# Values of the other half copied by ScalarE, chunk 22 through DRAM, and a new order: sliding-window attention with sinks and a gated layer, on one core

## The chip, the cores and the metric

The kernel runs on one core of a Trainium2 chip. The metric is the device time of one execution in microseconds (us), as the median over runs of the same program. In the text and in the rows PE is TensorE (PEld its weight loads, which overlap its matmuls), DVE is VectorE, ACT is ScalarE, POOL is GpSimd and SP is SyncE, which issues all of this kernel's transfers.

## The reference

Two parts, one behind the other. The first is attention over 4 batches x 8 heads x 768 positions x 64 elements, in which a position sees the last `window` = 128 positions and the first `n_sink` = 4:

```python
scores = np.matmul(q, k.transpose(0, 1, 3, 2)) / np.sqrt(D)
keep = (pos[None, :] < n_sink) | ((rel >= 0) & (rel < window))
scores = np.where(keep, scores, -1e9)
a = np.exp(scores - scores.max(-1, keepdims=True))
x = np.matmul(a / (a.sum(-1, keepdims=True) + 1e-9), v)
```

The second takes the 3072 rows of 512 elements through a layer of 1024:

```python
h = x @ w_in
e = np.exp(h - h.max(-1, keepdims=True))
solu = h * e / (e.sum(-1, keepdims=True) + 1e-9)
ln = (solu - mu) / np.sqrt(var + 1e-6) * g_ln
out = ln @ w_out
```

`w_in`, `w_out` and `g_ln` come as 8-byte floating-point numbers and are converted in the kernel.

## The kernel before

The 3072 rows are worked in 24 chunks of 128, six for each batch; the chunks (0, 0) and (1, 0) come first, then the others batch by batch. Every chunk passes the same stages, each a small function:

- `load_k`, `load_q`, `load_v` bring the inputs. Chunks 0 to 6 have q and k turned on PE (`turn_q`, `turn_k`, `take_q`, `take_k`); from chunk 7 on VectorE turns them in blocks of 32 (L539, L552).
- `score` (L579) multiplies q with the keys of the chunk before, the sinks and the chunk itself, `pick` and `mask` (L596, L609) choose and mask on VectorE, `exps` (L618) is on ScalarE, and `normalise` (L639) on POOL.
- From chunk 5 on the weights p are turned by way of DRAM: `store_p`, `load_p`, `flip_p` (L667, VectorE). POOL then cuts them into the parts that belong to the new and the old values (`part_new` L692, `part_old` L705).
- `value` (L760) multiplies the parts with the values. For a chunk that is not the first of its batch (17 chunks from chunk 5 on) it works by quarters and needs the values of the other half of the partitions too: the tile `vm`, of which there is one buffer, holds the upper half of the old values in its lower partitions and the lower half of the new ones in its upper partitions. `load_mid` (L504) fills it with two transfers from SBUF to SBUF.
- `x_hi` (ScalarE) and `x_lo` (VectorE) split the result in a high and a low part, `hidden` (L799) multiplies them with the first weights: 8 steps of three matmuls. `highest` (L804), `solu_exp` (L809), `solu` (L814), `centre` (L827, L830) and `square` are the gating and the norm.
- The product u must be turned. For most chunks it goes through DRAM: `store_u`, `load_u` (four transfers), `flip_u` (L856, two on VectorE). For the first and the last chunks, those that `direct(n)` names, PE turns it: `turn_u`, four steps of two transposes (L865).
- `u_hi` (L872), `u_lo` (L876), `project` (L890, 8 steps of three matmuls; 16 narrow ones for chunk 23), `scale`, `store`.

At the start the weights are converted in 16 blocks: ScalarE lowers them (L386), VectorE moves the bits (L390, L394, L400), and high and low parts are made, those of the second weights by `w_hi` on ScalarE and `w_lo` (L429) on VectorE.

The scores, the turned q and k, the turned p, the `value` results and the turned u share two PSUM buffers (`banks`). The hidden product `h` has one buffer: `hidden` of a chunk can begin when `solu` of the chunk before has read it.

The order of the work is written out by hand: `steps` lists every function call of every chunk, and the table `ORDER` says in which order they are recorded. Each engine, SP too, works through its instructions in that order, and one that waits holds up those behind it.

Of the kernel before, what the change touches and what calls it, by code (L numbers as in the profile page):

```python
# [184 lines left out]
def _banded(ctx, tc, q, k, v, n_sink, window, w_in, w_out, g_ln, out, val, wts, wpool, consts):  # L185
# [314 lines left out]
    def load_mid(n, i):  # L500
        if ("vm", n) not in st:
            st["vm", n] = sb.tile([P, H, D], F32, tag="vm", name=f"vm_{n}", bufs=1)
        src = st["vn", n] if i else old_values(n)
        nc.sync.dma_start(st["vm", n][ROWS[i]], src[ROWS[1 - i]])  # L504
# [336 lines left out]
    def direct(n):  # L841
        return n < 2 or n >= NCH - 2
# [272 lines left out]
```

## Time and profile before

| | |
|---|---|
| median of 3 runs | 410.08 us (409.6 to 411.29) |
| the profiled execution | 409.73 us |
| its span | 408.0 us, 12392 instructions |
[...]
| busy: PE, PEld | 388.5 us (95%), 308.9 us (76%) |
| busy: VectorE, ScalarE, POOL | 302.5 (74%), 254.2 (62%), 168.7 us (41%) |
| moved by DMA | 80.82 MB |

The span is the time from the first to the last instruction; 1.7 us of the execution lie around it. Busy shares are means over stages with different limits, so the sections below read them stretch by stretch. The granted clock is half of full speed in one stretch only, between 18.6 and 25.4 us, and at the very end.

### The profile page before, as it was taken

The numbers are of one execution on the slowest core, as the hardware profiler recorded it, in microseconds if no ns is written. First come the engines' busy times: TensorE is split into PE (matmuls) and PEld (weight loads), VectorE is DVE, ScalarE is ACT, GpSimd is POOL, SyncE is SP. The second block draws the span as 40 slices with busy tenths as digits, with TensorE's granted clock in tenths as the row PEclk, the third lists the DMA queues.
The fourth block names the chain that finished last, engine by engine and source line by source line (L and its number), as shares of the span: only waits on it lengthen the run. The fifth ranks groups of instructions, "written<-read, shape, count | busy, mean of one in ns | idle before, by whom it ended". The sixth has DMA issues, their size and how long they took to land.

```text
span 408.0 us, 12392 instructions
## 1 busy us (share of the span) xinstructions
PE 388.5 (95%) x4772; PEld 308.9 (76%) x4772; DVE 302.5 (74%) x883; ACT 254.2 (62%) x698; POOL 168.7 (41%) x312
## 2 busy tenths in 40 slices
PE   3799999989989999999999999999999999999995
PEld 3564767777777887878778878888888888888885
DVE  3889999999989898987989788775645836444320
ACT  3989998874968586538557847475445445342532
POOL 6622262645463954561246763542824421010100
PEclk9979999999999999999999999999999999999999
DMA  7999539969969969889957897998686341452011
GB/s 236 308 275 319 142 81 199 178 209 242 239 178 285 225 213 286 240 182 199 307 177 246 233 236 234 259 260 241 180 243 207 106 141 77 144 167 90 28 51 58
DMA packets 83316, 80.82 MB, mean 198 GB/s; under 512 B 45868, under 2 KB 66740, under 8 KB 83252
## 3 DMA queue, kind: packets, MB, share of 16 engines
q1 hardware_dynamic: 83252, 79.98, 72.4%
q8 instruction: 39, 0.64, 0.7%
q14 instruction: 25, 0.20, 0.2%
HBM read 48.76 MB, written 26.87 MB: 185 GB/s over the span
## 4 chain that ended last, share of the span: by engine, by line
PE 76%; DVE 10%; ACT 5%; POOL 2%; issue 2%; DMA 2%; SPq 1%; DVEq 0%; ACTq 0%; POOLq 0%
PE o L890 30%; PE h L799 28%; PE banks L579 7%; PE banks L760 6%; DVE w2l L429 2%; DVE sc L609 2%; ACT sc L618 1%; PE av L770 1%; DMA wraw<-in_moe_w_in_dram 1%; POOL pt L705 1%; DVE keys L552 1%; POOL pc L692 1%; DVE wbits L400 1%; PE banks L676 1%; ACT wps L386 1%
## 5 line engine op out<-in xcount | busy, mean ns | idle before, releaser
L618 ACT ACTIVATE sc<-sc,nmx 128x132 f32<-128x132 f32 x192 | 75.6, 398 | 17.8 <-DVE nmx L609 17.5
L890 PE MATMUL o<-w2h,uh 128*128 128x512 f32 (+1 forms) x200 | 79.3, 397 | 0.0
L799 PE MATMUL h<-w1h,xh 128*128 128x512 f32 x192 | 77.8, 405 | 0.0
L890 PE MATMUL o<-w2l,uh 128*128 128x512 f32 (+1 forms) x200 | 77.1, 386 | 0.1
L890 PE MATMUL o<-w2h,ul 128*128 128x512 f32 (+1 forms) x200 | 77.1, 386 | 0.0
L799 PE MATMUL h<-w1h,xl 128*128 128x512 f32 x192 | 75.6, 394 | 0.0
L799 PE MATMUL h<-w1l,xh 128*128 128x512 f32 x192 | 75.3, 392 | 0.0
L639 POOL TENSOR_TENSOR pn<-sc,rs 128x512 f32<-128x512 f32 x38 | 42.1, 1122 | 24.0 <-DVE rs L624 9.5
L809 ACT ACTIVATE e<-h,nm 128x1024 f32<-128x1024 f32 x24 | 26.8, 1117 | 35.1 <-DVE nm L804 34.9
L609 DVE CUSTOM_DVE_ANT_0 sc<-banks,bias 128x132 f32<-128x132 f32 x192 | 46.3, 286 | 2.9 <-POOL sn L646 0.6
L692 POOL TENSOR_SCALAR_AFFINE_SELECT pc<-pt 64x512 f32<-64x512 f32 x34 | 26.7, 785 | 49.3 <-DVE pt L667 48.2
L890 PEld LDWEIGHTS o<-w2h,uh 128*128 128x128 f32 x200 | 37.6, 188 | 9.8 <-issue 1.5
L890 PEld LDWEIGHTS o<-w2h,ul 128*128 128x128 f32 x200 | 37.5, 187 | 8.5 <-issue 0.3
L799 PEld LDWEIGHTS h<-w1h,xh 128*128 128x128 f32 x192 | 36.1, 188 | 10.2 <-issue 2.4
L804 DVE TENSOR_REDUCE nm<-h 128x1 f32<-128x1024 f32 x24 | 29.2, 1216 | 19.5 <-PE h L799 19.3
L890 PEld LDWEIGHTS o<-w2l,uh 128*128 128x128 f32 x200 | 37.5, 188 | 7.3
L876 DVE TENSOR_TENSOR ul<-ur,uh 128x512 fp32r<-128x512 f32 x40 | 28.3, 717 | 19.6 <-ACT uh L872 19.6
L579 PE MATMUL banks<-keys,q 32*64 32x200 f32 (+3 forms) x1280 | 39.0, 336 | 3.8 <-ACT keys L560 1.5
L799 PEld LDWEIGHTS h<-w1h,xl 128*128 128x128 f32 x192 | 36.1, 188 | 8.1
L799 PEld LDWEIGHTS h<-w1l,xh 128*128 128x128 f32 x192 | 36.2, 188 | 7.0
L579 PEld LDWEIGHTS banks<-keys,q 32*64 32x64 f32 (+1 forms) x1280 | 28.4, 135 | 13.3 <-issue 4.4
L872 ACT CAST uh<-ur 128x512 fp32r<-128x512 f32 x40 | 24.1, 614 | 21.7 <-DVE ur L856 16.5
(154 smaller groups left out, 745.8 us busy)
## 6 DMA issues: line engine op xcount, KB each, us to landing
ud<-u SPq DMA_DIRECT2D x20, 512.0 KB, 4.2
ub<-ud SPq DMA_DIRECT2D x80, 128.0 KB, 3.7
pd<-pn SPq DMA_DIRECT2D x19, 512.0 KB, 4.2
pb<-pd SPq DMA_DIRECT2D x76, 128.0 KB, 4.2
vn<-in_v_dram SPq DMA_DIRECT2D x24, 256.0 KB, 4.6
out_dram<-ob SPq DMA_DIRECT2D x23, 256.0 KB, 2.6
kn<-in_k_dram SPq DMA_DIRECT2D x12, 384.0 KB, 6.7
qn<-in_q_dram SPq DMA_DIRECT2D x12, 384.0 KB, 7.1
```

Of the source, the lines that this page charges most:

```text
L579: nc.tensor.matmul(st["s", n, g][ROWS[y], x, 256 * j + at:256 * j + at + wide], st["q", n][rows, m, ROWS[y]], kk[rows, m].rearrange("p b x ...
L609: nc.vector.tensor_tensor_reduce(out=st["sc", n][:, h], in0=st["s", n, g][:, x, 256 * j + BLK:256 * j + BLK + SEG], in1=bias0 if c == 0 el ...
L618: nc.scalar.activation(sc[:, h], sc[:, h], AF.Exp, bias=nmx[:, h:h + 1], scale=-1.0, accum_out=ssum[:, h:h + 1])
L639: nc.gpsimd.tensor_tensor(to[:, i], st["sc", n][:, :, PARTS[i]].rearrange("p h (b x) -> p h b x", x=32), st["rs", n].unsqueeze(2).unsqueez ...
L692: nc.gpsimd.affine_select(st["pc", n][ROWS[hb]].rearrange("p h (c t) -> p h c t", c=2), old_part(n)[ROWS[hb]], pattern=[[0, H], [32, 2], [ ...
L760: nc.tensor.matmul(acc[ROWS[x], y, r, :], vals[ROWS[y], h, :], p[ROWS[y], h, :], start=False, stop=(r, i) == (NPAIR - 1, 2))
L799: nc.tensor.matmul(st["h", n][:, cols], a[:, kt, :], w[:, kt, cols], start=(kt == 0 and m == 0), stop=(kt == KT1 - 1 and m == 2))
L804: nc.vector.tensor_reduce(nm, st["h", n], axis=AX.X, op=ALU.max, negate=True)
L809: nc.scalar.activation(e, st["h", n], AF.Exp, bias=st["nm", n], scale=1.0, accum_out=se)
L872: nc.scalar.copy(uh, turned_u(n, g4))
L876: nc.vector.tensor_tensor(ul, turned_u(n, g4), st["uh", n, g4].bitcast(F32), op=ALU.subtract)
L890: nc.tensor.matmul(st["o", n, i], a[:, kt % 4, :], part(w, kt)[:, i * wide:(i + 1) * wide], start=(kt == 0 and m == 0), stop=(kt == KT2 - ...
```

## The change

Three things. `load_mid` copies by ScalarE what two transfers moved. `direct` no longer names chunk 22, so that only chunk 23 of the last ones is turned on PE, and chunk 22 has `store_u`, four `load_u` and two `flip_u` in place of four `turn_u`. And the table `ORDER` is another one throughout (2021 steps instead of 2018). Of the table two lines stand here for all.

```diff
 ORDER = (
-    143, 12, 3, 0, 5, 6, 13, 144, 146, 8, 10, 11, 15, 16, 17, 147, 148, 149, 282, 150, 151, 18, 19, 21, 153, 4, 20,
...
         src = st["vn", n] if i else old_values(n)
-        nc.sync.dma_start(st["vm", n][ROWS[i]], src[ROWS[1 - i]])
+        nc.scalar.copy(st["vm", n][ROWS[i]], src[ROWS[1 - i]])
...
     def direct(n):
-        return n < 2 or n >= NCH - 2
+        return n < 2 or n >= NCH - 1
```

What the new table moves is seen in the order of the instructions on an engine. In the rows the number behind a tile's name is the chunk (for `wps`, `wraw` and `wbits` the weight block), the last number a running one.

ScalarE at the start, before:

```order
L226 CAST ident_r_93<-ident_88 128x128
L273 COPY val_58<-spread_0_144 128x2
L386 ACTIVATE wps_0_183<-wraw_0_181 128x512
L556 COPY q_0_190<-banks_0_86 128x512
L560 COPY keys_122<-banks_0_86 128x4x2x64
L416 CAST w1h_62<-wbits_0_211 128x4x128
L404 ACTIVATE minus_218<-ident_88 128x128
```

and after the change:

```order
L226 CAST ident_r_93<-ident_88 128x128
L404 ACTIVATE minus_137<-ident_88 128x128
L386 ACTIVATE wps_0_152<-wraw_0_135 128x512
L273 COPY val_58<-spread_0_148 128x2
L416 CAST w1h_62<-wbits_0_174 128x4x128
L556 COPY q_0_181<-banks_0_86 128x512
L560 COPY keys_122<-banks_0_86 128x4x2x64
```

The cast of the first weight block (L416), which needs VectorE's three steps on that block, stands ahead of the copies of q and keys of chunk 0 instead of behind them. On SP the fetch of that block is now the first transfer.

VectorE ahead of `hidden` of chunk 5, whose `h` buffer is free when `solu` of chunk 4 (L814) has run, before:

```order
L667 STREAM_TRANSPOSE pt_6_1742<-pb_6_1385 128x1024
L609 ISA sc_10_1648,nmx_10_1649<-banks_1_87,bias2_111 128x132
L609 ISA nmx_10_1649 128x1
L856 STREAM_TRANSPOSE ur_2_0_1761<-ub_2_1677 128x512
L804 TENSOR_REDUCE nm_4_1765<-h_4_1618 128x1
L731 TENSOR_TENSOR skt_6_1769<-skp_6_1753,mine_119 128x512
L609 ISA sc_10_1648,nmx_10_1649<-banks_1_87,bias2_111 128x132
L609 ISA nmx_10_1649 128x1
L784 TENSOR_TENSOR xl_5_1774<-banks_0_86,xh_5_1767 128x2x4x64
L814 SCALAR_TENSOR_TENSOR u_4_1811,nmu_4_1812<-h_4_1618,e_4_1808 128x1024
L856 STREAM_TRANSPOSE ur_2_1_1828<-ub_2_1677 128x512
```

and after the change:

```order
L609 ISA sc_10_1656,nmx_10_1657<-banks_1_87,bias2_111 128x132
L609 ISA nmx_10_1657 128x1
L552 STREAM_TRANSPOSE keys_122<-kn_2_1340 128x4x2x16 x4
L804 TENSOR_REDUCE nm_4_1718<-h_4_1583 128x1
L552 STREAM_TRANSPOSE keys_122<-kn_2_1340 128x4x2x16 x4
L784 TENSOR_TENSOR xl_5_1782<-banks_0_86,xh_5_1779 128x2x4x64
L731 TENSOR_TENSOR skt_6_1786<-skp_6_1777,mine_119 128x512
L814 SCALAR_TENSOR_TENSOR u_4_1828,nmu_4_1829<-h_4_1583,e_4_1825 128x1024
```

Two key transposes (of the third batch, chunks 13 and 14) now stand in this stretch, the `flip_u` of chunk 2 stands behind it, and the masks of chunk 10 all stand ahead of the sinks of chunk 6 (L731).

ScalarE between the `value` results of chunks 8 and 9 (their `x_hi`, L776), before:

```order
L776 CAST xh_8_2432<-banks_1_87 128x2x4x64
L618 ACTIVATE sc_13_2117,ssum_13_2119<-sc_13_2117,nmx_13_2118 128x132 x4
L872 CAST uh_3_1_2462<-ur_3_1_2362 128x512
L618 ACTIVATE sc_14_2309,ssum_14_2311<-sc_14_2309,nmx_14_2310 128x132 x6
L776 CAST xh_9_2543<-banks_1_87 128x2x4x64
```

and after the change:

```order
L504 COPY vm_8_2382<-vn_8_2272 64x512
L504 COPY vm_8_2382<-vn_7_1879 64x512
L618 ACTIVATE sc_13_2150,ssum_13_2152<-sc_13_2150,nmx_13_2151 128x132 x4
L776 CAST xh_8_2448<-banks_1_87 128x2x4x64
L872 CAST uh_3_0_2454<-ur_3_0_2380 128x512
L504 COPY vm_9_2465<-vn_9_2032 64x512
L504 COPY vm_9_2465<-vn_8_2272 64x512
```

The copies of chunk 9 stand behind `x_hi` and `u_hi` and can begin when `value` of chunk 8 has read the one `vm` buffer.

## Rows read from the trace of the kernel before

**Rows 1.** The page, part 1: busy us (share of the span) and instructions

```profile
PE 388.5 (95%) x4772; PEld 308.9 (76%) x4772; DVE 302.5 (74%) x883; ACT 254.2 (62%) x698; POOL 168.7 (41%) x312
```

**Rows 2.** Busy time by stretch; columns in the first line

```profile
core 0: us, PE busy (x) PEld busy (x) DVE busy (x) ACT busy (x) POOL busy (x), PEclk, DMA share, GB/s
...
10.40:84.60 74.20, 67.50 (x810) 48.73 (x802) 70.07 (x225) 67.38 (x200) 31.27 (x53) 0.95 0.87 215
84.60:115.00 30.40, 29.37 (x474) 23.15 (x474) 28.80 (x114) 21.82 (x76) 14.90 (x27) 1.00 0.94 221
115.00:170.00 55.00, 54.90 (x938) 43.95 (x938) 51.28 (x177) 37.19 (x122) 31.91 (x53) 1.00 0.83 244
170.00:330.00 160.00, 159.36 (x2184) 129.25 (x2185) 118.58 (x312) 93.31 (x248) 74.44 (x125) 1.00 0.82 221
```

**Rows 3.** The chain that ended last: start us, us, what

```profile
81.88 0.68 DVE ul L876
82.64 0.59 ACT uh L872
...
84.64 1.61 PE banks L579 x64
...
359.97 0.87 PE banks L865 x8
...
374.74 9.08 PE o L890 x39
```

**Rows 4.** Waits from 84 to 408 us: who for whom, us, times, longest

```profile
PEld banks L760 <- POOL pt L705: 1.4, 4, 0.5
...
PE banks L579 <- POOL d L819: 1.2, 1, 1.2
```

**Rows 5.** Timeline of the start: start us, us, engine, line, operation, tiles [idle before]

```profile
2.55 1.05 SPq L374 DMA_DIRECT2D wraw<-in_moe_w_in_dram  x2
...
7.44 0.63 ACT L386 ACTIVATE wps<-wraw 128x512 f32<-128x512 f32 x1 [1.39 <-DMA wraw<-in_moe_w_in_dram]
...
8.10 0.70 DVE L390 TENSOR_SCALAR wps<-wps 128x512 int32<-128x512 int32 x1 [2.37 <-ACT wps L386]
8.48 0.58 ACT L560 COPY keys<-banks 128x512 f32<-128x512 f32 x1
...
10.46 0.29 DVE L609 CUSTOM_DVE_ANT_0 sc<-banks,bias 128x132 f32<-128x132 f32 x1 [0.21 <-POOL bias L279]
```

**Rows 6.** VectorE, groups by form (count, busy us, mean ns), and one timeline row

```profile
L856 DVE STREAM_TRANSPOSE ur<-ub 128x512 f32<-128x512 f32 x40 | 27.0, 694 | 5.7 <-issue 3.5 <-DMA ub<-ud 2.1
...
L552 DVE STREAM_TRANSPOSE keys<-kn 128x128 f32<-128x128 f32 x72 | 19.3, 392 | 0.0
...
113.51 0.69 DVE L731 TENSOR_TENSOR skt<-skp,mine 128x512 fp32r<-128x512 f32 x1 [0.77 <-PE skp L726]
```

**Rows 7.** ScalarE's cast out of SBUF; the `vm` transfers; SP's waits for them

```profile
L872 ACT CAST uh<-ur 128x512 fp32r<-128x512 f32 x40 | 24.1, 614 | 21.7 <-DVE ur L856 16.5 <-PE o L890 4.3 <-DVE rs L623 0.9
...
vm<-vn SPq DMA_DIRECT2D x33, 128.0 KB, 3.2
...
SPq L504 <- PE banks L760: 20.5, 5, 4.8
```

**Rows 8.** `w_lo` on VectorE (ns min/median/max), one of them, POOL at that time

```profile
L429 DVE SCALAR_TENSOR_TENSOR w2l<-wbits,g_sb,w2h x8: 666/887/1535, 52.0 to 79.4; 128x512 fp32r<-128x512 f32 x8
...
79.36 1.47 DVE L429 SCALAR_TENSOR_TENSOR w2l<-wbits,g_sb,w2h 128x512 fp32r<-128x512 f32 x1
...
79.23 2.50 POOL L639 TENSOR_TENSOR pn<-sc,rs 128x512 f32<-128x512 f32 x2
```

**Rows 9.** Transfers of u (us to landing), and the product's row

```profile
ud<-u SPq DMA_DIRECT2D x20, 512.0 KB, 4.2
ub<-ud SPq DMA_DIRECT2D x80, 128.0 KB, 3.7
...
L814 DVE SCALAR_TENSOR_TENSOR u<-h,e 128x1024 f32<-128x1024 f32 x24 | 29.3, 1221 | 8.6 <-ACT e L809 8.1
```

195 rows, old and new, of the table ORDER are left out of this document.

## The prediction

> **What bounds the kernel now.** I read the busy shares first, then busy time by stretch, then the chain of waits, then single instructions. PE is busy for 95% of the span [rows 1], but that figure is too kind: matmuls are pipelined, and one that waits still counts as busy. The weight loads beside it are a better gauge [rows 2]. Per microsecond PEld works 48.73/74.20 = 0.66 from 10.4 to 84.6 us, 0.76 up to 115 us, 0.80 up to 170 us and 0.81 from there to 330 us. So PE is truly full only in the later part. In the same rows VectorE is busy for 70.07 of 74.20 us, 28.80 of 30.40 and 51.28 of 55.00, and then for only 118.58 of 160.00. The kernel therefore has two limits, one after the other: up to about 115 us VectorE (with ScalarE close behind, 67.38 of 74.20), and PE behind it; from about 170 us PE alone; between them both.
>
> The chain says the same [rows 3]. Up to then it runs over VectorE and ScalarE (a low part at 81.88, a high part at 82.64); at 84.64 us it enters PE with the scores of chunk 7, and from there it is PE nearly to the end. PE's waits from 84 us on are few [rows 4]: 1.2 us before the scores of chunk 7, and 1.4 us of weight loads in four places before a `value`, for POOL's masked weights. A full PE costs 9.08/39 = 0.233 us per matmul of 512 columns [rows 3], so 0.70 us for one step of `project` or `hidden` (three matmuls). An edit can help in three ways only: less PE work, an earlier handover at 84.64 us, or fewer of these waits.
>
> **The change part by part.**
>
> *Chunk 22 through DRAM.* Its four `turn_u` steps go, eight transposes on PE. The row of one chunk is 0.87 us for eight, in a stretch where PE has nothing else [rows 3]: **-0.87 us**. Added are one store, four loads, two `flip_u` on VectorE and the DRAM round trip. From the last `hidden` of chunk 22 to its first `project` the new order has 37 steps of 0.70 us, 25.9 us. The round trip is: maximum, exp, product and centring, four passes over 1024 columns at 1.22 us, the product's row, 4.9; store 4.2 and load 3.7 [rows 9]; two flips at 0.69 [rows 6], 1.4; high and low part at about 0.65, 1.3: 15.5 us. SP issues the fourth load behind the stores of chunks 19 and 16; `project` of chunk 16 ends 19 steps (13.3 us) ahead of chunk 22's first, and scaling, issue, load, flips and halves take about 8.5 us after it. Cost nothing, covered by other `project` steps; without that cover the 15.5 us would show in part.
>
> *The values of the other half.* SP loses 34 issues, each with 3.2 us to landing; ScalarE gains 34 copies of 64 x 512 elements. The trace has no such copy; its nearest row is the cast of 128 x 512 out of SBUF on ScalarE, 614 ns [rows 7]. I take 0.61 us (half the partitions need not halve it), 20.9 us in all; the low bound is 0.3 us each. ScalarE is idle for 55.00 - 37.19 = 17.8 us from 115 to 170 us and for 66.7 us from 170 to 330 us [rows 2], so as a sum they fit. What matters is who stands behind them. The tightest place is chunk 9: PE has four `hidden` steps (2.8 us) between the `value` of chunks 8 and 9, and in that time ScalarE must do `x_hi`, `u_hi` and two copies, four times 0.61, 2.4 us. It just fits. Cost 0, bound +0.5 us at each of the two places of this kind (chunks 9 and 14), nothing gained by the copies themselves.
>
> On SP the gain is indirect. A transfer into `vm` has to wait for PE to finish with it (one buffer), and SP stood still 20.5 us for that in five waits [rows 7], with loads and stores of the weights queued behind. PE's late waits for POOL's masked weights come at the end of such a sequence (SP, load, flip, mask). I credit the 1.4 us of [rows 4]: **-1.4 us**; bounds 0 and -2.6 us (both rows).
>
> *The start.* SP now fetches the first weight block first. Before, it was issued at 2.55 us and its conversion began at 7.44 us [rows 5], 4.9 us later. Issued at 0.8 us it can begin at 5.7 and end at 6.3. But ScalarE then has the cast of that block ahead of the copies of q and keys, and that cast waits for three VectorE steps, 2.2 us (8.10 to 10.3): 8.5 us, cast to 9.1, two copies to 10.2. Before, the copies ended at 9.06 and the first mask began at 10.46 us. With the same 1.4 us between, it begins at 11.6: **+1.1 us** on VectorE, which has no spare time to give it back before 84 us. Bounds: 0 (faster landing) and +1.5.
>
> *The order on VectorE.* In the stretch before `hidden` of chunk 5 two key transposes (chunks 13 and 14) have moved ahead; at 19.3/18 = 1.07 us each [rows 6] that is 2.1 us. One `flip_u` (0.69 [rows 6]) moves behind, and one transpose falls into a gap of 0.77 us that VectorE has there for the sinks of chunk 6 [rows 6]; 2.1 - 0.69 - 0.77 leaves 0.7, and half of it is lost again in the wait for `x_hi`, which both orders have: **+0.3 us**; bounds -1.0 (the whole wait before the scores of chunk 11 goes) and +2.1. Elsewhere the order hands over at nearly the same sum of work: before chunk 7's scores VectorE has the same steps within 1 us, and PE has done project steps ahead that it must wait for at chunk 8's scores, since q of chunk 8 stands behind the same VectorE work.
>
> *The low parts of the second weights.* Eight VectorE steps in the VectorE-bound stretch move to other neighbours. Their rows run from 0.67 to 1.54 us for the same shape, and the long one at 79.36 us lies under a POOL multiplication from 79.23 us [rows 8]. I keep their sum of 8.0 us; at the ends of the range it would be 5.3 or 12.3. [...]
>
> Sum: -0.87 - 1.4 + 1.1 + 0.3 = -0.9 us on the profiled execution's 409.73 us (span 408.0 and 1.7 around it): **408.9 us**. That execution is 0.35 us under the median of the three runs, 410.08, so the change would be about -0.3%. A measurement of this kernel can tell 0.5%, 2.05 us, from no change.
>
> **Rivals.**
>
> *VectorE's gaps close (faster).* The new order may fill what VectorE idles before the handover: 4.1 us from 10.4 to 84.6 and 1.6 us to 115 us [rows 2]. If half of that goes and the start costs nothing: 409.73 - 0.87 - 1.4 - 2.9 = 404.6 us; with two thirds of it, 403.7. For it: ScalarE and DMA are freed of nothing there, but weights and attention are interleaved anew. Against it: VectorE is already 94 to 95% busy, and its total work before the handover is the same to 1 us.
>
> *Early key transposes push PE back (slower).* Counted along the order, chunks 13, 14, 16 and 17 have their key transposes 9 to 29 us of VectorE work earlier, inside the stretch where VectorE is as scarce as PE. Four times 1.07 us before masks and `x_lo` that PE waits for, none of it absorbed: 409.73 - 0.87 + 1.1 + 4.3 = 414.3 us. VectorE's idle time of 3.7 us from 115 to 170 us can absorb most of it, and the sign turns once more than about 2 us of the 4.3 is not absorbed.
>
> *ScalarE's copies stand in the way (slower).* If a third of the 17 pairs, six times 1.2 us, delays an exp or `u_hi` that PE waits for by half its length, +3.7 us: 412.6 us. Against it: ScalarE idles a third of the time there.
>
> *POOL beside the low parts (slower).* At the upper end of [rows 8] their sum is 12.3 us instead of 8.0, +4.3 us: 413.2 us; that holds only if POOL runs beside nearly all eight. [...]
>
> **How the numbers follow.** Forecast, within 0.5%: 0.42. Gaps close: 0.37. Key transposes: 0.12. Copies in the way: 0.05. POOL beside the low parts: 0.04. So faster by over 0.5% 0.37, same 0.42, slower 0.21. The range goes from 403.6 (two thirds of the gaps) to 413.5 us (most of the key transposes, or either of the other two); the likeliest case alone has 407.5 to 411.
>
> **What would show it.** Right: the handover to PE within 1.5 us of 84.64, the first mask near 11.6 us, PEld share from 115 us on unchanged, eight records fewer on L865, no `vm` issue on SP, copies of about 0.6 us on ScalarE. Wrong: a handover 3 us earlier with VectorE idle far below 4 us in 10 to 85 us; or masks and `x_lo` as releasers of PE between 115 and 170 us, with more idle time of PEld there; or ScalarE's copies in the chain; or the chain's end waiting on chunk 22's loads.

## The result, and the profile after

The changed kernel took 414.4 us in the median of four runs (413.07 to 415.91), the kernel before 410.33 us (409.6 to 411.29) beside it: a ratio of 1.0104, 95% interval 1.008 to 1.0128. It is slower by about 1%, and outside the range of 403.6 to 413.5 us. In a second series, again with the kernel before beside it, the same kernel had 412.36 us over twelve runs, from 407.83 to 414.83, where the kernel before stayed between 408.2 and 411.42: slower by 0.4% there (ratio 1.0011 to 1.0069), and less steady. Medians in this document are over all runs, while ratios leave out those more than 1.5% above the fastest of their kernel (two of these twelve).

The profiled execution took 413.07 us, its span 411.4, against 409.73 and 408.0. The page, part 1, of the changed kernel:

```profile
PE 388.4 (94%) x4764; PEld 308.6 (75%) x4764; DVE 306.0 (74%) x885; ACT 275.4 (67%) x732; POOL 167.8 (41%) x312
```

Against [rows 1], ScalarE has 34 instructions and 21 us more, PE eight transposes less, and no engine is near a new limit. By stretch, with the columns of [rows 2] (the last three: granted clock of TensorE, DMA share, GB/s):

```profile
10.40:84.60 74.20, 67.12 (x790) 48.49 (x782) 70.86 (x229) 65.70 (x196) 33.53 (x55) 0.95 0.86 225
84.60:115.00 30.40, 29.68 (x544) 23.75 (x545) 29.34 (x118) 22.83 (x78) 14.30 (x26) 1.00 0.94 228
115.00:170.00 55.00, 52.96 (x886) 42.18 (x871) 49.81 (x168) 42.51 (x126) 30.09 (x47) 0.97 0.74 207
170.00:330.00 160.00, 159.14 (x2005) 128.28 (x2004) 117.14 (x309) 106.75 (x275) 71.74 (x127) 1.00 0.75 203
```

In PE's column one row differs by more than a trifle: from 115 to 170 us PE is busy for 52.96 us and no longer 54.90, at a granted clock of 0.97. So I read the chain of waits there (start us, us, what):

```profile
111.02 1.60 PE banks L760 x96
...
113.26 0.70 DVE xl L784
...
114.00 1.57 PE banks L579 x53
115.57 2.04 issue
117.61 0.55 PE banks L579 x3
...
118.37 4.41 PE h L799 x12
```

L760 is the `value` of chunk 5, L579 the scores of chunk 11, L799 `hidden` of chunk 5. PE had done 61 of the 64 score matmuls when it stood still for 2.04 us, with three left, and "issue" says that no semaphore held it. From the end of that `value` to `hidden` it is 118.37 - 112.62 = 5.75 us here, and 116.86 - 113.26 = 3.60 in the kernel before, whose chain has no such gap:

```profile
111.70 1.56 PE banks L760 x96
...
114.46 0.57 PE banks L579 x8
...
115.06 1.58 PE banks L579 x56
...
116.86 3.57 PE h L799 x15
```

Then, in the changed kernel, 12 matmuls of `hidden` took 4.41 us where 0.233 each [rows 3] gives 2.8: the granted clock of TensorE was half for a while (0.50 from 118.7 to 121.9 us, which is 0.62 as a mean from 119 to 123, below). I count that to the gap: in the profiles in which PE was busy for 3.91 us or more of the 4 from 115 to 119 (the kernel before and seven of the runs below; here it was 1.96) the clock was 1.00 from 115 to 123 us, while two others in which PE stood longer there (busy for 2.82 and 2.57 us) had 0.83 and 0.79 from 119 to 123. Half the clock did not follow every gap: those of 0.95 and 1.24 us at other places, in two of the runs below, had 1.00 behind them. Together that is +3.8 us (2.15 and 1.6), a little more than the whole difference of the spans, 3.4.

What else runs at that time? SyncE's issues in the timeline of the changed kernel (start us, us of issue, line, tiles, count):

```profile
106.52 0.34 SPq L653 DMA_DIRECT2D pd<-pn  x1
106.96 1.17 SPq L660 DMA_DIRECT2D pb<-pd  x1
108.18 0.44 SPq L474 DMA_DIRECT2D qn<-in_q_dram  x1
108.67 0.47 SPq L851 DMA_DIRECT2D ub<-ud  x1
109.23 0.40 SPq L486 DMA_DIRECT2D vn<-in_v_dram  x1
109.68 0.58 SPq L851 DMA_DIRECT2D ub<-ud  x1
110.35 0.38 SPq L846 DMA_DIRECT2D ud<-u  x1
112.83 0.34 SPq L653 DMA_DIRECT2D pd<-pn  x1
113.22 1.74 SPq L660 DMA_DIRECT2D pb<-pd  x3
115.05 1.53 SPq L486 DMA_DIRECT2D vn<-in_v_dram  x1
```

The kernel before, in nearly the same stretch:

```profile
105.25 0.34 SPq L653 DMA_DIRECT2D pd<-pn  x1
105.64 2.09 SPq L474 DMA_DIRECT2D qn<-in_q_dram  x3
113.32 1.51 SPq L504 DMA_DIRECT2D vm<-vn  x2
```

There SP stood at the `vm` transfer and issued nothing for more than 5 us. Its DMA share (before first, the changed kernel behind it):

```profile
112.00:115.00 3.00, 2.01 (x97) 1.46 (x87) 2.23 (x5) 2.50 (x7) 1.72 (x4) 1.00 0.73 135
115.00:119.00 4.00, 3.96 (x71) 3.25 (x68) 3.78 (x17) 2.21 (x11) 3.29 (x6) 1.00 0.49 165
```

```profile
112.00:115.00 3.00, 2.28 (x97) 1.78 (x92) 2.82 (x8) 2.36 (x7) 1.72 (x4) 1.00 1.20 299
115.00:119.00 4.00, 1.96 (x28) 1.16 (x13) 1.34 (x6) 3.13 (x13) 2.51 (x4) 0.95 1.00 312
119.00:123.00 4.00, 4.00 (x17) 3.10 (x16) 3.50 (x21) 1.51 (x2) 0.29 (x1) 0.62 0.57 130
```

And the DMA queues of the changed kernel from 115.0 to 116.2 us (packets, MB, share) hold something that is no data of the kernel:

```profile
q1 hardware_dynamic: 136, 0.45, 94.7%
q8 instruction: 1, 0.02, 5.4%
```

One packet of 16 KB on q8 begins at 115.11 us, when PE is at its last matmuls before the gap, and takes 1.04 us; PE goes on 1.46 us behind its end. From 111 to 115 us there is none. Over the run q8 has 39 such packets, about one per 250 of PE's 9,528 matmuls and weight loads. So I take them for PE's program; the run with the shifted stream, below, shows it.

Two smaller things. VectorE waited 3.22 us for keys of batch 3, whose load took 8.43 us to land (transfers of this kind have a median of 7.3 on the page), and PE stood 0.75 us behind it before the scores of chunk 17. And the end is longer: the last scaling starts at 405.88 us of 411.4, before at 403.77 of 408.0. The records of L166, where the program ends, show SP's last branch and the waits behind it (count, ns, first and last start us), first of the kernel before, then of the changed one:

```profile
L166 SPq EVENT_SEMAPHORE  x8: 17/17/17, 405.2 to 406.2; - x8
...
L166 SPq COMPARE_BRANCH  x1: 50/50/50, 404.7 to 404.7; - x1
```

```profile
L166 SPq EVENT_SEMAPHORE  x8: 17/17/17, 409.4 to 410.0; - x8
...
L166 SPq COMPARE_BRANCH  x1: 50/50/50, 406.8 to 406.8; - x1
```

From the branch to the first wait it was 0.5 us, and now 2.6: the span's end comes 1.3 us later for it, counted from the last scaling (5.5 us against 4.2).

### The profile page after: what moved, and what is told of

Its sections match the earlier page's. It is cut to its first block, busy times and chain, and to the rows that moved or that the text cites. A ratio compares the mean times of both kernels' runs of the same rounds, so it can differ in the third digit from the quotient of the medians.

```text
span 411.4 us, 12400 instructions
## 1 busy us (share of the span) xinstructions
PE 388.4 (94%) x4764; PEld 308.6 (75%) x4764; DVE 306.0 (74%) x885; ACT 275.4 (67%) x732; POOL 167.8 (41%) x312
## 4 chain that ended last, share of the span: by engine, by line
PE 70%; DVE 8%; ACT 8%; POOL 4%; DMA 3%; issue 3%; SPq 2%; DVEq 0%; ACTq 0%; POOLq 0%
PE o L890 29%; PE h L799 26%; PE banks L579 6%; PE banks L760 5%; DMA kn<-in_k_dram 3%; ACT sc L618 2%; PE av L770 1%; DVE sc L609 1%; DVE wbits L400 1%; DVE nm L804 1%; ACT u L830 1%; PE banks L676 1%; PE banks L743 1%; PE banks L865 1%; DVE w2l L429 1%
## 5 line engine op out<-in xcount | busy, mean ns | idle before, releaser
L799 PE MATMUL h<-w1h,xh 128*128 128x512 f32 x192 | 78.3, 408 | 0.0
L799 PE MATMUL h<-w1h,xl 128*128 128x512 f32 x192 | 76.4, 398 | 0.0
L799 PE MATMUL h<-w1l,xh 128*128 128x512 f32 x192 | 75.9, 395 | 0.0
L639 POOL TENSOR_TENSOR pn<-sc,rs 128x512 f32<-128x512 f32 x38 | 40.5, 1076 | 43.0 <-DMA pd<-pn 13.8
L876 DVE TENSOR_TENSOR ul<-ur,uh 128x512 fp32r<-128x512 f32 x42 | 30.9, 739 | 20.7 <-ACT uh L872 20.7
L579 PE MATMUL banks<-keys,q 32*64 32x200 f32 (+3 forms) x1280 | 40.0, 335 | 5.7 <-issue 2.0
L872 ACT CAST uh<-ur 128x512 fp32r<-128x512 f32 x42 | 25.7, 615 | 28.2 <-DVE ur L856 16.1
L799 PEld LDWEIGHTS h<-w1h,xh 128*128 128x128 f32 x192 | 36.6, 190 | 10.1 <-issue 2.2
L692 POOL TENSOR_SCALAR_AFFINE_SELECT pc<-pt 64x512 f32<-64x512 f32 x34 | 25.8, 761 | 43.5 <-DVE pt L667 42.4
L799 PEld LDWEIGHTS h<-w1h,xl 128*128 128x128 f32 x192 | 36.4, 190 | 8.5 <-DVE xl L788 0.2
L799 PEld LDWEIGHTS h<-w1l,xh 128*128 128x128 f32 x192 | 36.5, 190 | 7.2
L579 PEld LDWEIGHTS banks<-keys,q 32*64 32x64 f32 (+1 forms) x1280 | 28.4, 134 | 16.2 <-issue 6.2
```

Of the source, the lines that this page charges most:

```text
L579: nc.tensor.matmul(st["s", n, g][ROWS[y], x, 256 * j + at:256 * j + at + wide], st["q", n][rows, m, ROWS[y]], kk[rows, m].rearrange("p b x ...
L639: nc.gpsimd.tensor_tensor(to[:, i], st["sc", n][:, :, PARTS[i]].rearrange("p h (b x) -> p h b x", x=32), st["rs", n].unsqueeze(2).unsqueez ...
L692: nc.gpsimd.affine_select(st["pc", n][ROWS[hb]].rearrange("p h (c t) -> p h c t", c=2), old_part(n)[ROWS[hb]], pattern=[[0, H], [32, 2], [ ...
L799: nc.tensor.matmul(st["h", n][:, cols], a[:, kt, :], w[:, kt, cols], start=(kt == 0 and m == 0), stop=(kt == KT1 - 1 and m == 2))
L872: nc.scalar.copy(uh, turned_u(n, g4))
L876: nc.vector.tensor_tensor(ul, turned_u(n, g4), st["uh", n, g4].bitcast(F32), op=ALU.subtract)
```

## The experiments

Theories. **Backlog**: SP issues other transfers earlier, and PE's instructions come late behind them. **Order**: the new order of VectorE's work makes PE wait. **Copies**: ScalarE's copies stand in the way. Edits of the order are shown by the names of the steps, as SP has them.

**The changed kernel again** (no edit).

> The changed kernel once more, nothing altered, for a second profile and more times. In its first profile PE stood for 2.04 us among the scores of chunk 11 (115.57 to 117.61 us) with no releaser, while a transfer of PE's own instructions ran at 115.11 us, and TensorE's clock was 0.62 from 119 to 123 us. Backlog theory (SP, no longer held by the vm transfers, issues other transfers earlier, and PE's instructions come late behind them): the gap without a releaser comes back at the same place, 1 to 3 us long, and the time is 413 to 416 us. Order theory (key transposes and a late key load): no such gap, but waits of PE of 1.5 us and more behind VectorE near the scores of chunk 17, 413 to 416 us. If neither is in the profile, both were accidents of one execution.

Measured: 412.36 us, ratio 1.004 (1.0011 to 1.0069). The gap came back between the same two matmuls of the chain, 2.18 us long:

```profile
114.17 1.57 PE banks L579 x53
115.74 2.18 issue
117.92 0.55 PE banks L579 x3
```

So it was no accident of one execution. But both profiled executions have a low mean granted clock, 0.984 and 0.985 (the kernel before 0.991 in its profile), while the six fastest of these twelve runs had 0.992 to 0.997 (407.83 to 411.52 us). No profile shows whether the gap is in those, so the 3.8 us are its cost in the two profiled executions, not in every run.

**The transfers of `vm` back on SP, in the new order.**

```diff
-        nc.scalar.copy(st["vm", n][ROWS[i]], src[ROWS[1 - i]])
+        nc.sync.dma_start(st["vm", n][ROWS[i]], src[ROWS[1 - i]])
```

> The changed kernel with the one line of load_mid put back: SP transfers instead of ScalarE copies, everything in the new order. Backlog theory: SP is held again until PE has read vm, DMA is quiet near 113 us (share about 0.5 and not 1.09), the gap in the scores of chunk 11 is gone, and the time falls to 409.5 to 412 us, unless the transfers, placed for ScalarE, come late for their value (2.8 us of PE work at chunk 9 against 3.2 us of landing), which can cost 0.5 us at each of two places. Copies-in-the-way theory: ScalarE loses 20.9 us of copies, waits of PE for it go, 410 us. Order theory: unchanged, 413 to 416 us.

Measured: 422.98 us, ratio 1.032 (1.0295 to 1.0344). All three expectations failed. PE's waits from 84 to 330 us (who for whom: us, times, longest):

```profile
PE banks L760 <- DMA vm<-vn: 5.2, 4, 3.5
PE banks L579 <- issue: 1.4, 2, 1.3
```

The new order leaves too little time between one `value` and the next for a transfer of 3.2 us; it rests on copies of 0.62 us. These waits are 5.2 of the some 11 us that the run lost to the changed kernel; where the rest went is open. And the gap in the scores of chunk 11 stays (1.28 us), though `vm` is SP's again: in the new order SP issues the same transfers of q, u and v ahead of it, from 106.71 to 109.85 us, and the next one into `vm` only at 115.25 us. So it is the place that the new order gives SP's other steps, not the freeing of SP, that brings the burst.

**ScalarE's copies alone, in the order of before.** The 34 steps of `load_mid` moved to places where ScalarE idled, which I chose from the trace.

> The kernel before with the ScalarE copies alone: its order is kept, only the 34 steps of load_mid move to places where ScalarE idles between one value and the next. Backlog theory: SP runs ahead here too, DMA share near 113 us rises from 0.53 towards 1, PE loses 2 us and more there or at a like place: 411.5 to 414 us. Copies-in-the-way theory: also slower, but with PE waiting for ScalarE. Order theory: no slower than before, 408.5 to 410.5 us, since the waits of PE for masked weights (1.4 us) go and nothing is added.

Measured: 413.1 us, ratio 1.0075 (1.0055 to 1.0094). The DMA share from 112 to 119 us fell to 0.47 and 0.33 instead of rising, so the backlog theory's reason for this run was wrong: in the old order SP, freed of `vm`, issued nothing from 107.5 to 116.4 us either. PE waited in small pieces, among them 1.8 us of weight loads for POOL's masked weights, where [rows 4] had 1.4: freeing SP does not end those waits. Since the places were mine and not those of the change, the 3.1 us are no price of the copies; what they come from is open.

**Five SP steps later.**

```diff
 load_p.7 (1)
-load_q.12 (2), load_u.2 (0), load_v.6, load_u.2 (2), store_u.3
 store_p.9
+load_u.2 (0), load_u.2 (2), load_q.12 (2), load_v.6, store_u.3
 load_p.7 (3), load_p.8 (0), load_p.7 (2)
```

> The changed kernel with five SP steps moved on SP alone: two loads of u of chunk 2, one load of q of chunk 12, the values of chunk 6 and the store of u of chunk 3 are issued behind the store of the weights of chunk 9 (112.83 us) and not at 108.2 to 110.4 us. Backlog theory: PE's instructions, wanted near 111.6 us, meet a quiet DMA, the 2.04 us gap at 115.57 us and the half clock behind it go, 2 to 3.6 us less than the changed kernel: 410.5 to 412.5 us; if the later transfers only move the backlog, a gap appears at the next transfer of instructions instead. Order theory: no change, 413 to 416 us, or slower, as project of chunk 2 waits.

Measured: 412.12 us, ratio 1.0058 (1.0032 to 1.0083). DMA was quiet (share 0.02 from 109 to 112 us), PE's instructions began to move at 110.93 us, and the gap in the scores was gone. The time stayed near the changed kernel's (1.004 beside it), though: I had delayed the values of chunk 6 as well, which took 7.2 us to land:

```profile
PE banks L760 <- DMA vn<-in_v_dram: 3.4, 1, 3.4
```

**Four SP steps later**, as above without `load_v.6`.

> The changed kernel with four SP steps moved on SP alone behind the store of the weights of chunk 9: two loads of u of chunk 2, one load of q of chunk 12 and the store of u of chunk 3; the values of chunk 6 stay where the change has them (the run before this one moved them too, and PE stood 3.58 us for them at 117.29 us). Backlog theory: neither the gap without a releaser in the scores of chunk 11 (2.04 and 2.18 us in two profiles) nor the wait for the values of chunk 6 is there, and PE gains what both runs lost: 3 to 5 us under the changed kernel's 412.4 us of the last job, 407.5 to 409.5 us. Rival (PE loses these microseconds here in any order, since chunk 5's low part is late): PE still waits 3 us and more between the scores of chunk 11 and hidden of chunk 5, 411 to 414 us.

Measured: 408.61 us, ratio 0.9953 (0.9935 to 0.997), as the backlog theory has it. Four steps moved on SP, nothing on any engine that computes, and about 1% is back (the changed kernel had 1.0104 and 1.004). PE goes through the 56 scores of chunk 11 without a gap:

```profile
113.87 1.58 PE L579 MATMUL banks<-keys,q 32*64 32x200 f32 x56 [0.72 <-DVE xl L784]
```

The DMA queues from 111.5 to 113.5 us hold PE's instructions alone:

```profile
q8 instruction: 1, 0.02, 3.2%
```

**The key loads earlier too**: `load_k.18` (3) and (0) moved from 169.8 us to behind (2) and (1) at 149 us.

> The run above, with the last two loads of the keys of batch 3 moved on SP from 169.8 us to behind the first two at 149.0 us. In two profiles of the changed kernel these loads landed 8.4 us after issue, VectorE's key transposes of chunk 18 waited for them, and PE with them before the scores of chunk 17: 1.5 and 0.9 us. If that is a cost of the change, it goes: 0.8 to 1.5 us under the run above, 406.5 to 408.5 us. If PE only waits elsewhere instead, the same time as the run above.

Measured: 409.25 us, ratio 0.9983 (0.9969 to 0.9996). The wait before the scores of chunk 17 went, and a new gap without a releaser came, in `hidden` of chunk 8, behind the new burst:

```profile
155.06 0.46 PE h L799 x2
155.52 1.24 issue
156.75 3.37 PE h L799 x14
```

I had made the same fault at another place.

**The key loads in SP's idle time**, behind `load_p.11` (1): 157.7 us by the changed kernel's times, 152.85 us in this run.

> The changed kernel with the four SP steps moved (408.61 us in the last job) and the last two loads of the keys of batch 3 issued at 157.7 us on SP, where it stands idle till 165.2 us, and not at 149.0 us, where they ran into the fetch of PE's instructions (PE stood 1.6 us in hidden of chunk 8 at 155.13 us, no releaser). Backlog theory: neither that gap nor the wait before the scores of chunk 17 (1.0 us) is there; 407 to 408.3 us. Rival (DMA is late there wherever the loads stand): a gap of 1 us and more is left at one of the two places, 408.3 to 409.5 us.

Measured: 407.75 us, ratio 0.994 (0.9918 to 0.9963). Of PE's waits from 84 us on a single one is left in that view:

```profile
PE banks L579 <- DVE xl L784: 0.7, 1, 0.7
```

This version beats both kernels: it is the change with six steps of SP moved. From the version with four (0.9953) it is not told apart: the intervals overlap.

**Chunk 22 through PE again**, on the version with the four steps (and, as a run of its own, on the one with the early key loads).

```diff
-        return n < 2 or n >= NCH - 1
+        return n < 2 or n >= NCH - 2
```

In `ORDER` the four `turn_u` of chunk 22 replace the seven steps of its way through DRAM.

> The changed kernel with the four SP steps moved, and u of chunk 22 through PE again. With the key loads moved as well the same edit took 2.1 us in the medians, but its profile had other differences (1.5 us until the scores of chunk 7). My forecast: 0.87 us for eight transposes, so 409.2 to 409.9 us against 408.61 us. If PE also waits before the first project of chunk 22, as it did for 0.65 us at 391.53 us, up to 410.3 us; if the way through DRAM brings nothing, 408.6 us.

> The run above (four SP steps and the key loads moved), with u of chunk 22 through PE again, as before the change: eight transposes more on PE. My forecast put 0.87 us on them, hidden in nothing: 0.6 to 1.1 us slower than the run above. If the way through DRAM costs PE something near its end, the same time or faster.

Measured: 410.27 us, ratio 1.0007 (0.9981 to 1.0033), against 0.9953: 0.54%, 2.2 us; and 411.34 us, 1.0034, against 0.9983, 2.1 us. By the intervals each pair leaves 1 to 3 us or so. Besides the eight transposes PE waits 0.4 us (its weight loads 0.8) in the first `project` of chunk 22, for the low part behind them; the rest is not seen in the two profiles. I had put 0.87 us on this part of the change. The run with the early key loads has the gap in `hidden` of chunk 8 again, 0.94 us at 157.06 us.

**Two idle transfers added to the kernel before**, 512 KB each, behind its last load of q of chunk 12.

> The kernel before with two transfers added on SP behind its last load of q of chunk 12 (107.5 us): 512 KB each from q to DRAM that nobody reads, where its DMA was quiet otherwise. Backlog theory: the transfer of PE's instructions, at 113.08 us in the kernel before, starts later, PE stands without a releaser in the scores of chunk 11 or just behind them, 1 to 3 us, perhaps with half the clock behind it: 411.5 to 414 us. Rival: PE waits there only for VectorE and ScalarE, as before, and the transfers are covered: 409.5 to 411 us.

Measured: 409.75 us in the median, ratio 1.0014 (0.9984 to 1.0044), but with four of twelve runs at 414.2 to 416.4, where the kernel before had none over 410.83 in 29. The profiled run was one without the loss: DMA share 1.11 from 112 to 115 us, and PE's instructions still came at 113.35. So a busy DMA alone does not make that transfer late. Whether the four runs lost their 4 to 7 us to it, no profile shows.

**PE's instruction stream shifted, no transfer touched.** The transposes of the weights of chunk 3 are done twice.

```diff
-                for i in range(2):
+                for i in (0, 1, 0, 1) if n == 3 else (0, 1):
```

> The changed kernel with nothing moved and no transfer touched, but 64 transposes of the weights of chunk 3 (53 us) done twice, each into the same place with the same result: 128 instructions more on PE (64 matmuls and their weight loads, 1.08 us by the profile). If the gap of 2.04 to 2.18 us in the scores of chunk 11 is PE waiting for its own instructions, whose transfer meets the burst of SP's transfers of 106 to 115 us, then PE asks for that transfer 128 instructions earlier in the program, before the burst, and the gap goes: 409.5 to 411.5 us, 1 us of which the added work may take. If the gap is something else that SP's transfers do to PE, it stays: 412.5 to 415.5 us.

Measured: 413.33 us, ratio 1.0073 (1.0049 to 1.0096). The gap in the scores of chunk 11 is gone, with DMA as busy as in the changed kernel (share 1.19 from 112 to 115 us); PE's instructions now moved at 107.98 us. But further on, where the stream had moved too, a gap of the same kind came in the `value` of chunk 8, two matmuls before its end:

```profile
145.47 1.55 PE banks L760 x94
147.02 0.95 issue
147.97 0.34 PE banks L760 x2
```

The time did not improve, so the number in the expectation was wrong. The place decides it, though: a gap that moves when only PE's own instruction count moves is PE waiting for its instructions.

Counting shows it more sharply. Number PE's records in a trace (matmuls, weight loads and waits) in order of their start. After the first 10 us, seven of the profiles have nine gaps of PE over 0.1 us without a releaser, and behind them stands record 2753 (three times), 3777, 4034, 4289 (twice), 6082 or 6337: always a multiple of 256 apart, give or take one. In all nine PE goes on 1.2 to 1.6 us behind the end of a packet on q8. In the changed kernel PE reaches record 2497, where the 256 ahead of the gap begin, at 111.41 us, and the packet starts 3.7 us later; with the four steps moved it starts 0.6 us after that point, in the kernel before 1.0 us.

**SP's stream made longer again**: 34 transfers of 256 bytes, with the stores of chunks 16 to 19 on the version with the four steps, then, on the best version, only where no load stands behind them.

> The changed kernel with the four SP steps moved, and 34 transfers of 256 bytes added on SP with the output stores of chunks 16 to 19, where SP has nothing to do: as many instructions more as the change took from SP's stream. In all five profiles of the new order with ScalarE copies SP's first wait behind its last branch ends 2.5 to 2.9 us after the branch; in the kernel before, and with the new order and the 34 transfers of vm, 0.5 us after it. If the length of SP's stream is what does it (the instructions behind the branch are fetched late), that wait falls to about 0.5 us and the time by 1 to 1.5 us, 407 to 407.8 us. Rival (the last store lands later in the new order): the tail stays, 408.3 to 409.3 us.

> The version with the four SP steps moved and the key loads at 157.7 us (407.75 us in its job), and 34 transfers of 256 bytes on SP again, now only where nothing stands behind them: 10 behind the store of chunk 19, 12 behind the last load of u of chunk 22, 8 and 4 behind the stores of chunks 20 and 22. With the padding PE's end is not touched, and SP's first wait behind its last branch, 2.9 us in that version, falls to 0.5 us as in the padded run: span 1.3 to 1.6 us shorter, 406.0 to 406.7 us. If the tail hangs on something else, or the padding costs as much, 407.3 to 408.5 us.

Measured: 421.04 us, ratio 1.0266 (1.0226 to 1.0306), and 409.54 us, 0.9987 (0.9965 to 1.0009). Neither time was as expected: in the first the padding (0.6 us a transfer) held back loads of u that PE needed, in the second one of the last stores of the output took 2.23 us to issue behind it, where 0.33 is usual. The wait behind SP's branch did fall, as expected, to 0.5 and 0.8 us.

It is not the count of transfers alone: the copies in the order of before have 34 fewer and kept 0.5 us, and the version with chunk 22 through PE has as few and waits 2.5. That the branch's place in SP's stream decides fits all of these; no run shows it by itself.

## Why the prediction was wrong

**The step that failed** is the term for the stretch before `hidden` of chunk 5, "**+0.3 us**; bounds -1.0 (the whole wait before the scores of chunk 11 goes) and +2.1". I counted that stretch on VectorE alone, and for the rest I wrote "Elsewhere the order hands over at nearly the same sum of work". For SP I counted only what it no longer waits for. What SP issues at the places that the new order gives it, and what that collides with, stood in the sum at nothing, without a reason. The runs showed in its place +3.8 us in that very stretch: 2.04 us of PE standing without instructions (2.18 in the second profile) and 1.6 us at a lower clock (0.62). Without the gap it is 5.75 - 2.04 = 3.71 us from `value` to `hidden`, against 3.60 before, so on VectorE the term was about right.

Moving four of SP's steps took the collision out: 408.61 us. That this is next to the forecast of 408.9 is luck, since the terms below were off in both directions. No rival of mine had this mechanism, and 414.3 us for the early key transposes is the right size for a wrong reason: VectorE's transposes of chunks 13 and 14 did come 11 and 19 us earlier, they are as early in the version at 407.75 us, and PE's only wait there is the 0.7 us shown above.

Term by term:

*Transposes, -0.87.* Mis-sized: 2.1 to 2.2 us in two pairs of runs, each uncertain by about 1 us. The way through PE also makes `project` of chunk 22 wait, for 0.4 us, which is part of the difference; the rest is open.

*PE's waits for POOL's weights, -1.4.* The size was nearly right, the reason wrong. The row of [rows 4] went from 1.4 us in four waits to this, in the changed kernel:

```profile
PEld banks L760 <- POOL pt L705: 0.2, 1, 0.2
```

But with the copies alone the waits stayed, at 1.8 us, and with the new order and `vm` on SP there is one of 1.4 us: neither part of the change ended them by itself.

*The start, +1.1.* Mis-sized. The first mask begins at 10.66 us and not 11.6, against 10.46 [rows 5]; this is 0.2 us. The first weight block landed sooner than I took it to (conversion at 4.50 us, not 5.7), and its cast was done by the time q and keys were ready. Nor was the path the one I summed: by its row the first mask waited for POOL's `bias`, as it did before [rows 5], and not for the copies of q and keys. The first two rows are of ScalarE, the third of VectorE:

```profile
4.50 0.62 ACT L386 ACTIVATE wps<-wraw 128x512 f32<-128x512 f32 x1 [1.89 <-DMA wraw<-in_moe_w_in_dram]
...
7.49 0.62 ACT L416 CAST w1h<-wbits 128x512 fp32r<-128x512 f32 x1 [1.19 <-DVE wbits L400]
```

```profile
10.66 0.30 DVE L609 CUSTOM_DVE_ANT_0 sc<-banks,bias 128x132 f32<-128x132 f32 x1 [2.41 <-POOL bias L279]
```

*The copies, 0 at 0.61 us each.* Right: 0.62 us each, and PE never waited for one.

```profile
L504 ACT COPY vm<-vn x33: 616/618/622, 95.3 to 349.7; 64x512 f32<-64x512 f32 x33
```

*The low parts of the second weights, 8.0 us.* Right: 7.5 us in sum, eight with a median of 883 ns (887 before [rows 8]), 675 to 1531. That POOL's work beside them sets their length no run shows: in both kernels seven of the eight ran beside POOL, for 666 to 1535 ns before and 744 to 1531 now, and the eighth without it for 743 and 675 ns; the sums of 8.0 and 7.5 us are far from the 12.3 us of the rival with POOL.

*VectorE, +0.3, and the handover.* PE began the scores of chunk 7 at 85.6 us, 1 us later than before, inside the 1.5 us that I gave it. By 84.6 us it had done 12 matmuls of `project` more (2.8 us at 0.233 each) and 32 narrow ones of a `value` (L770) less (1.9 us), which makes up for it: nothing in sum. Of VectorE's gaps 0.8 us of 4.1 closed (70.86 us busy from 10.4 to 84.6, 70.07 before), and the handover came no earlier, so that rival, with 0.37 the likeliest of them, was wrong too.

*Not in the sum at all:* the key loads of batch 3 (0.75 us of PE's standing in the first profile; in the medians, 0.9953 and 0.994, not told from noise) and the longer end (1.3 us). Both are SP's as well.

With these sizes in place of mine, an estimate for the two profiled executions: -2.1 - 1.2 + 0.2 + 0.1 + 2.0 + 1.6 + 0.75 + 1.3 = +2.7 us, of the 3.4 by which the spans differ. The other 0.7 us are within what is uncertain in the transposes.

## What to carry to other kernels

When a change frees a queue or re-orders it, list what that queue issues in the time gained, and at its new places, and look at the DMA share there, not only at who no longer waits. A gap on an engine with "issue" as its only reason, in the middle of a run of short instructions, is looked up among the instruction packets of the DMA queues: here the cure was to move four transfers some 4 us back, behind the packet of PE's instructions (it started at 111.9 us in that run, the first of the four was issued at 113.23). And a cure by moving transfers is read at the place they are moved to, twice here a new wait.

## What the runs showed of the hardware

As I read these runs, PE's program comes in packets of 16 KB on q8 (39 in a run of 4,764 matmuls and as many weight loads), and PE can outrun them: nine gaps of 0.16 to 2.18 us, at records whole multiples of 256 apart. PE ran through the 256 records ahead of each in 4.2 to 6.7 us, since most of them were of scores or a `value`, where a matmul and its load take 0.016 to 0.025 us instead of 0.233. There a packet that started 2.1 to 4.8 us after PE had reached the first of the 256 was too late; ahead of the scores of chunk 11 one that started 0.5 to 1.1 us after it was in time. Transfers of data nearby can make the difference (3.7 us, and 0.6 with four of them moved), but a high DMA share alone did not (two idle transfers: share 1.11, and 0.8 us). What decides it beyond that is open.

SP's first wait behind its last branch (L166) came 2.6 us after it in the changed kernel and 0.5 us after it in the kernel before; what makes the difference is open.

A busy PE is not a full PE by these records: a matmul of 512 columns is recorded with 0.39 us where the next starts 0.23 us after it, and one that opens a series with 0.51 us, as at 86.18 us of the kernel before, where its record starts together with its own weight load of 0.19 us.
